# One decode step on one core: the first weight matrix in two loads, 16 partitions and 112

## The chip, the core and the metric

The kernel runs on one core of a Trainium2 chip. The metric is device time in microseconds of one execution; several runs are taken and their median is given. Separately, one execution is recorded by the hardware profiler.

## The reference

One token of a transformer block: grouped-query attention against a cache of 16384 positions, then a mixer and an MLP. Cut to what matters here:

```python
x = A_x                                       # (1, 1, 512)
q = layernorm(x) @ wq                         # wq: 512 x 4096, 32 heads of 128
k, v = repeat(k_cache, 4), repeat(v_cache, 4) # each (8, 16384, 128), bf16
p = softmax(q k^T / sqrt(128));  o = p v
h = x + o @ wo                                # wo: 4096 x 512
c = gelu(layernorm(layernorm(h)) @ w1); ...   # mixer: a shift in time and w2
x1 = ...
out = h + x1 + gelu(layernorm(x1) @ w3) @ w4  # w3: 512 x 1792, w4: 1792 x 512
```

With one token the mixer's shifts leave only zeros, so w1 and w2 are not loaded. The keys and values are 32 MB each and wq, wo are 4 MB each: nearly all the work is to bring bytes from device memory.

## The kernel before

Every operation is noted by a small class, `Program`, with the engine, the tiles that it reads and writes, and, for loads, a semaphore by name. `emit` then writes each engine's instructions in the order noted, with a wait wherever an operation needs a result of another engine or of a load (L101 is the line of the waits). So the order on each engine's queue is the order in the source. `load` (its DMA is issued at L225) puts a load on SP's queue, unless told otherwise; only the token itself, `x4`, is loaded by ACT.

The tiles: `kb` holds keys, 128 partitions by 64 KB, in two halves `kb[0]` and `kb[1]`; `vb` holds values, 128 by 64 KB; `kt` holds one half of the keys transposed. wq has no tile of its own: `wq_sb` is `vb`, whose first half holds wq until the first values come. Partition p of wq_sb gets rows 4p to 4p+3 of wq, which lie one after the other in memory: 32 KB a partition.

The heads are taken in four pairs j. For each pair and half y, DVE transposes the keys in eight pieces (L397) from `kb[y]` into `kt`, PE computes scores (L405), and when both halves are done comes the softmax (L416 to L437) and the product with the values (L448), gathered by DVE (L459, L462). `load_keys(j + 1, y)` is noted after the transposes of pair j, and SP waits at L101 until they are done; pair 1 is loaded as a whole. `load_values(j + 1)` waits for L448 of pair j. The loads of wo, w3 and w4 follow into `kb`.

At the start SP issues wq, then the two halves of the first keys, with no wait. Beside them ACT loads the token, DVE and POOL make constants, and the layernorm of the token is computed on DVE; its end is `xn` (L345). L378 are the 32 matmuls of the projection: they read `xn` and wq, 64 output partitions and 512 columns each, contracting over the 128 partitions, so that every one needs all partitions of wq. L382 and L388 bring the queries into the layout of the scores. `load_values(0)` stands behind: SP waits for the last of the L378 matmuls, since values overwrite wq. In the last pair and after it PE runs some spare matmuls (`spin`, L262) whose results are not used.

In the kernel before, the load of wq writes the key "v", the key of the loads of the values too.

## Time and profile before

| | |
|---|---|
| median of 3 runs | 191.53 us (191.33 to 191.57) |
| profiled execution, its own time | 191.19 us |
| its span, first to last instruction | 189.9 us |
| PE, DVE busy | 122.6 us (65%), 115.8 us (61%) |
| moved from device memory | 79.17 MB, mean 417 GB/s over the span |
| chain that ended last, by engine | DMA 61%, DVE 31%, PE 4% |
| wq: issue to landing | 4096 KB, 12.2 us |

The span is cut into 40 slices of 4.75 us. A digit gives the busy share in tenths; the GB/s row is what the 16 DMA engines of the core moved in that slice. In the chain, each line is a start, a duration and the work that held the end back then. An entry such as "DVE kt<-kb L397" names the engine, the tile written and the tile read.

### The profile page before, as it was taken

The numbers are of one execution on the slowest core, as the hardware profiler recorded it, in microseconds if no ns is written. First come the engines' busy times: TensorE is split into PE (matmuls) and PEld (weight loads), VectorE is DVE, ScalarE is ACT, GpSimd is POOL, SyncE is SP. The second block draws the span as 40 slices with busy tenths as digits, with TensorE's granted clock in tenths as the row PEclk, the third lists the DMA queues.
The fourth block names the chain that finished last, engine by engine and source line by source line (L and its number), as shares of the span: only waits on it lengthen the run. The fifth ranks groups of instructions, "written<-read, shape, count | busy, mean of one in ns | idle before, by whom it ended". The sixth has DMA issues, their size and how long they took to land.

```text
span 189.9 us, 1730 instructions
## 1 busy us (share of the span) xinstructions
PE 122.6 (65%) x726; PEld 45.9 (24%) x726; DVE 115.8 (61%) x176; ACT 9.4 (5%) x16; POOL 7.0 (4%) x15
## 2 busy tenths in 40 slices
PE   0129099693085004999449599944929998779893
PEld 0114033221032001342123222212313422334231
DVE  7755597993502007999450999935079897514274
ACT  3000000002000000000110000011000000500011
POOL 7100000000000000000000000000000000000032
PEclk9999969999558555799956999996575999999999
DMA  6999999999999999997999999999999999989992
GB/s 221 442 442 442 442 442 444 442 442 431 442 442 442 428 442 442 442 442 342 442 435 428 456 442 414 390 442 414 442 442 442 469 431 414 442 368 409 433 408 84
DMA packets 2610, 79.26 MB, mean 417 GB/s; under 512 B 298, under 2 KB 428, under 8 KB 556
## 3 DMA queue, kind: packets, MB, share of 16 engines
q1 hardware_dynamic: 2594, 79.17, 97.2%
q8 instruction: 5, 0.08, 0.2%
q14 instruction: 1, 0.01, 0.0%
q10 hardware_dynamic: 10, 0.00, 0.0%
HBM read 79.17 MB, written 0.00 MB: 417 GB/s over the span
## 4 chain that ended last, share of the span: by engine, by line
DMA 61%; DVE 31%; PE 4%; issue 1%; SPq 1%; ACT 1%; ACTq 0%
DMA kb<-in_A_k_cache_dram 46%; DVE kt L397 28%; DMA kb<-in_B_w_dram 14%; PE O_ps L448 3%; DVE pt L433 1%; SPq L225 1%; DVE mx L416 1%; ACT p_sb L429 1%; DVE od L462 1%; PE s_ps L405 1%; PE mn_ps L571 0%; DVE fin L577 0%; PE mn_ps L423 0%; PE mn_ps L419 0%; DVE od L459 0%
## 5 line engine op out<-in xcount | busy, mean ns | idle before, releaser
L405 PE MATMUL s_ps<-kt,qb 128*128 128x512 bf16 x256 | 69.5, 411 | 24.4 <-DVE kt L397 21.6
L397 DVE STREAM_TRANSPOSE kt<-kb 128x1024 int32<-128x1024 int32 x64 | 72.8, 1206 | 16.7 <-DMA kb<-in_A_k_cache_dram 16.7
L405 PEld LDWEIGHTS s_ps<-kt,qb 128*128 128x128 bf16 x256 | 22.8, 102 | 70.2 <-DVE kt L397 45.7
L448 PE MATMUL O_ps<-vb,pt 128*32 128x512 bf16 x256 | 21.9, 517 | 10.7 <-DMA vb<-in_A_v_cache_dram 6.3
L459 DVE TENSOR_SCALAR od<-O_ps,rowc 128x128 f32<-128x128 f32 x4 | 1.4, 350 | 28.0 <-PE O_ps L448 28.0
L448 PEld LDWEIGHTS O_ps<-vb,pt 128*32 128x32 bf16 x256 | 8.9, 125 | 22.5 <-issue 11.0
L433 DVE STREAM_TRANSPOSE pt<-p_sb 64x1024 bf16<-64x1024 bf16 x8 | 9.9, 1240 | 5.4 <-ACT p_sb L429 5.3
L262 PE MATMUL O_ps<-kt,qb 128*128 128x512 bf16 x52 | 12.9, 380 | 0.0
L429 ACT ACTIVATE p_sb<-s_ps,bias 128x1024 bf16<-128x1024 f32 x4 | 4.5, 1114 | 156.5 <-DVE nmh L425 156.5
L416 DVE TENSOR_REDUCE mx<-s_ps 128x1 f32<-128x1024 f32 x4 | 4.9, 1225 | 4.5 <-PE s_ps L405 4.5
L378 PE MATMUL O_ps<-vb,xn 128*64 128x512 bf16 x16 | 3.6, 631 | 5.8 <-DMA vb<-in_A_wq_dram 5.8
L315 POOL TENSOR_SCALAR st<-st 128x1 f32<-128x1 f32 x1 | 0.2, 244 | 177.5 <-DVE st L300 177.5
L262 PEld LDWEIGHTS O_ps<-kt,qb 128*128 128x128 bf16 x52 | 4.5, 99 | 6.0 <-issue 1.8
L465 PE MATMUL A_ps<-od,zz 128*128 128x128 f32 x8 | 2.0, 326 | 5.1 <-DVE od L462 5.1
L437 PE MATMUL A_ps<-acc,zz 128*128 128x1 f32 x8 | 1.6, 271 | 5.3 <-ACT p_sb L429 5.3
L462 DVE SCALAR_TENSOR_TENSOR od<-O_ps,rowc,od 128x128 f32<-128x128 f32 x12 | 4.2, 351 | 0.4
L419 PE MATMUL mn_ps<-ident_f,mx 128*1 128x128 f32 x8 | 1.5, 271 | 4.4 <-DVE mx L416 4.4
L337 DVE CAST quarter<-ident_f 4x128 bf16<-4x128 f32 x1 | 3.9, 3904 | 0.6 <-POOL ident_f L332 0.6
L339 PE MATMUL O_ps<-x,quarter 4*128 4x128 bf16 x1 | 0.3, 282 | 5.7 <-DVE quarter L337 5.7
L382 DVE STREAM_TRANSPOSE qcol<-O_ps 128x256 f32<-128x256 f32 x4 | 1.6, 428 | 3.9 <-PE O_ps L378 3.9
L378 PEld LDWEIGHTS O_ps<-vb,xn 128*64 128x64 bf16 x16 | 1.4, 167 | 7.2 <-DVE zz L367 5.9
L516 DVE COPY osum<-O_ps 128x512 f32<-128x512 f32 x1 | 0.7, 691 | 3.7 <-PE O_ps L509 3.7
(87 smaller groups left out, 50.9 us busy)
## 6 DMA issues: line engine op xcount, KB each, us to landing
kb<-in_A_k_cache_dram SPq DMA_DIRECT2D x6, 4096.0 KB, 23.5
vb<-in_A_wq_dram SPq DMA_DIRECT2D x1, 4096.0 KB, 12.2
kb<-in_A_wo_dram SPq DMA_DIRECT2D x1, 3072.0 KB, 27.2
kb<-in_B_w_dram SPq DMA_DIRECT2D x1, 1792.0 KB, 24.2
kb<-in_B_w_dram SPq DMA_DIRECT2D x1, 1280.0 KB, 27.0
kb<-in_A_wo_dram SPq DMA_DIRECT2D x1, 1024.0 KB, 29.2
kb<-in_B_w_dram SPq DMA_DIRECT2D x1, 384.0 KB, 27.4
kb<-in_B_w_dram SPq DMA_DIRECT2D x1, 128.0 KB, 27.3
```

The costliest lines, as they stand in the source:

```text
L225: P.op(by, lambda e: e.dma_start(dst, src), w=[key, *also], dma=name)
L262: pe(lambda e: e.matmul(O_ps[out][:, :], qb[:, 0, 0, 0:128], kt[:, 0:512], start=True, stop=True), r=["qb", ("kt", 0)], w=[("O", out)], ba ...
L337: dve(lambda e: e.tensor_copy(quarter[:, :, :], ident_f[0:4, 0:4].unsqueeze(2).to_broadcast([4, 4, 32])), r=["ident_f"], w=["quarter"])
L378: pe(lambda e, row=row, k=k, g=g, at=at: e.matmul(row[64 * g:64 * g + 64, :], copies(xn[:, k:k + 1], 64), wq_sb[:, at:at + REP * DH], star ...
L397: dve(lambda e, view=view: e.transpose(view(kt), view(kb[y])), r=[("r", y, n) for n in range(RPARTS)], w=[("kt", t)])
L405: pe(lambda e, n=n, c=c: e.matmul(s_ps[:, y, :], qb[:, n, j, QPAD - 4 * c:QW - 4 * c], ktv[:, n // 2, n % 2, :, 8 * c:8 * c + 8, :], start ...
L416: dve(lambda e: e.tensor_reduce(mx[:, :], s_all, AX.X, ALU.max), r=[("s", 0), ("s", 1)], w=["mx"], **both)
L429: act(lambda e: e.activation(p_sb[:, :], s_all, ACTF.Exp, bias=bias[:, 0:1], scale=float(SCALE), accum_out=acc[:, :]), r=[("s", 0), ("s", ...
L433: dve(lambda e, g=g: e.transpose(pt[64 * g:64 * g + 64, :, :, g, :], p_sb[64 * g:64 * g + 64, :]), r=["p"], w=["pt"])
L448: pe(lambda e, q=q, ct=ct, xl=xl, ch=ch: e.matmul(O_ps[j % 2][32 * ct:32 * ct + 32, :], pt[:, xl, ch, :, :].rearrange("p g u -> p (g u)"), ...
L462: dve(lambda e, block=block, c=c: e.scalar_tensor_tensor(od[:, :], block, rowc[:, c:c + 1], od[:, :], ALU.mult, ALU.add), r=[key, "rowc", ...
L465: pe(lambda e: e.matmul(A_ps[:, 0:128], zo[:, 96 - 32 * j:224 - 32 * j], od[:, :], start=False, stop=(j == PAIRS - 1), skip_group_check=True),
```

## The change

wq comes by two loads of SP in place of one: the first brings partitions 0 to 15, the second partitions 16 to 127. Both have semaphores and keys of their own. The projection matmuls wait for both; the loads of the values are marked as writing over both.

```diff
+WQ = ((0, 16), (16, 128))
...
         def load_values(j):
-            load("v", vb[:, :], pair_rows(A_v_cache, j), "v")
+            load("v", vb[:, :], pair_rows(A_v_cache, j), "v", also=[("wq", 0), ("wq", 1)])
...
-        load("wq", wq_sb[:, 0:NCH * HQ * DH], A_wq.rearrange("(p k) c -> p (k c)", k=NCH), "v")
+        wq_in = A_wq.rearrange("(p k) c -> p (k c)", k=NCH)
+        for n, (lo, hi) in enumerate(WQ):
+            load(f"wq{n}", wq_sb[lo:hi, 0:NCH * HQ * DH], wq_in[lo:hi, :], ("wq", n))
...
-                        start=(k == 0), stop=(k == NCH - 1)), r=["xn", "v"], w=[key], bank=[key])
+                        start=(k == 0), stop=(k == NCH - 1)), r=["xn", ("wq", 0), ("wq", 1)], w=[key], bank=[key])
```

The order of instructions on PE, DVE, ACT and POOL stays as it was; SP's queue has one load more, right behind the first.

## The prediction

> **What bounds the kernel now.** I read the page's transfer rows first, then the chain that ended last, then the start of the timeline, and last a table of small windows over the first two microseconds. The slices of the page:

> ```profile
> DMA  6999999999999999997999999999999999989992
> GB/s 221 442 442 442 442 442 444 442 442 431 442 442 442 428 442 442 442 442 342 442 435 428 456 442 414 390 442 414 442 442 442 469 431 414 442 368 409 433 408 84
> ...
> q1 hardware_dynamic: 2594, 79.17, 97.2%
> ...
> vb<-in_A_wq_dram SPq DMA_DIRECT2D x1, 4096.0 KB, 12.2
> ```

> From the second slice to the last but one the 16 DMA engines are busy, at the same 442 GB/s for wq, keys and values, whatever the compute engines do. 79.17 MB at 442 GB/s is 179.1 us of the span of 189.9. The rest is a head, where nothing moves yet, and a tail of compute. The chain says the same with the order of things:

> ```profile
> 0.72 0.40 SPq L225
> 1.12 0.06 issue
> 1.17 0.42 SPq L225
> 1.59 0.05 issue
> 1.64 31.49 DMA kb<-in_A_k_cache_dram
> 33.15 9.14 DVE kt L397 x8
> ...
> 160.02 27.42 DMA kb<-in_B_w_dram
> ...
> 187.48 0.64 PE mn_ps L571 x8
> 188.14 0.41 DVE fin L577
> ```

> The first link is SP's issue of the wq load, then that of the keys. A piece of keys issued at 1.64 lands 31.49 us later, not because it is slow but because 4 MB of wq and 4 MB of keys stand ahead of it on the same engines. DVE's transposes (L397) wait for those landings, and all later loads wait for the buffers that DVE and PE give back. Nowhere in the middle does the stream run dry (DMA share 7 to 9 tenths in every slice), so a delay of the stream at its head has no gap to disappear in: it arrives at the end in full. The same holds for a gain. And a load has landed only when the slowest of the 16 engines has brought its share, so it is the slowest lane that counts. The windows show the head:

> ```profile
> 1.60:1.70 0.10, 0.00 (x0) 0.00 (x0) 0.01 (x1) 0.10 (x1) 0.10 (x2) 1.00 0.04 8
> 1.70:1.80 0.10, 0.00 (x0) 0.00 (x0) 0.10 (x1) 0.10 (x1) 0.10 (x1) 1.00 6.32 1641
> ...
> 1.90:2.00 0.10, 0.00 (x0) 0.00 (x0) 0.10 (x1) 0.10 (x1) 0.10 (x1) 1.00 3.49 983
> ```

> The last two columns are the DMA share and GB/s; a packet is counted whole where it starts, so shares above 1 are rows that begin there. wq's rows begin from about 1.7, some 0.6 us after SP finished issuing at 1.12, and all lanes have begun by about 2.1.

> **The unit of the sum.** wq is 4096 KB, 128 rows of 32 KB, 8 rows to an engine. At 442 GB/s it takes 9.49 us, so one row on one lane takes 9.49 / 8 = 1.19 us (27.6 GB/s a lane). I call that a row-time.

> **Part by part.** *One more issue on SP.* The rows of L225 on SP last 0.33 to 0.43 us, so the second wq load goes out at about 1.6, and the two key loads at 1.64 and 2.1 move back by some 0.45 us. Behind them SP has nothing until the value load at 18.88. The cover is the wq transfer itself, 9.49 us: the keys' rows cannot start before it is through. The first load alone holds each lane one row-time, to about 2.9, and the second load's rows should be there by 1.6 + 0.6 = 2.2. Cost zero; without that cover, 0.45 us.

> *One more completion.* Each load ends with one small marker on each lane. The page has 2594 packets on the queue for 18 loads by SP, and 442 GB/s holds across loads of 4 MB and 8 MB alike, so a marker costs too little to see: zero, at most 0.05 us.

> *The extra wait on PE.* L378's first matmul waits for two loads instead of one. Behind it on PE stand the 32 projection matmuls, and DVE's L382 and SP's value load wait for them. The larger load lands last on the lanes, so the wait for the small one is over by then: zero. SP's value load waits for the same L378 matmuls as before.

> *Earlier first bytes.* Bounded by the head: the wq issue took 0.398 us against 0.328 for most others, and rows begin 0.6 us after it. If a load of 16 rows is prepared faster than one of 128, at most about 0.4 us is won; at least nothing. I take 0, since short and long loads (the 128 KB one too) show issues of 0.33 to 0.43.

> *Where the 16 rows land.* This decides. Every load so far writes all 128 partitions, so the trace shows 442 GB/s only for transfers spread over the whole width of SBUF. The change sends 16 engines at 16 neighbouring partitions, an eighth of the width. If the 27.6 GB/s of a lane is a limit of the engine or of the source, the 16 rows take one row-time, 1.19 us, and nothing changes. If it is a limit of the place of landing, and an eighth of the partitions takes an eighth of the rate, they take 8 row-times, 9.49 us. These are the ends from the rows. That the rate is the same 442 for 32 KB rows of keys and 64 KB rows of values, from different tensors and beside any compute, speaks for a fixed width on this side of the transfer. Whole loads run evenly with eight rows to a lane, so the nearest reading of these rows is 16 entries of one lane-rate, each serving the eight partitions of one lane. How the eight are grouped no row shows: as eight neighbours the 16 rows meet on two entries (9.49 us), as two groups of four on four entries, four lanes to each (4 row-times, 4.75 us), as pairs on eight (2.4 us). [...]

> [...] It ends at 4 + 11 = 15 row-times instead of 8. The loads behind it are even again, so it catches nothing up and stays 7 row-times late: 7 x 1.19 = 8.3 us. [...] The least under any sharing by four is 4 row-times (the 12 untouched entries still have 8 rows each, after the first 4): 4.7 us. In pairs the first load loses one row-time and the second little: 1.2 us or more. Lanes that start unevenly can drag each other for up to about five row-times more: some 14 us.

> **Sum.** 0 + 0 + 0 + 8.3 on the profiled execution's 191.19 us (span 189.9 and 1.3 around it) is 199.5; on the median of the runs, 191.53, it is 199.8. Own range 196 to 206.

> **Rivals.** (1) *Faster: the limit is not at the landing, and the small load starts the stream sooner.* For it: 0.6 us lie between issue and first row, and the stream's start is on the chain, so a gain is kept to the end. Against it: issues cost the same at every size. It decides if a lane writes anywhere at 27.6 GB/s; then the time is 191.53 less up to 0.4, some 191.2, or unchanged. (2) *It doesn't do what it says:* the rows are given to engines by where they land, so four engines take four rows each and the second load gives these four fewer. All lanes then carry 8 rows as before and the time stays at 191.5. [...] (3) *Only the first load pays:* the 112 rows run evenly, 3 row-times lost, 191.5 + 3.6 = 195.1. [...] (4) *The 112 rows are dealt in turn,* so every step lands on 16 neighbours: 8 steps lose 3 row-times each, 28.6 us, 220.

> **Chances.** Forecast 0.55, rival 1 0.15, rival 2 0.12, rival 3 0.10, rival 4 0.08. A measurement can tell about 0.2% here, 0.4 us. Rival 1 splits into faster 0.06, same 0.06, slower 0.03 (small costs without the gain); rival 2 into 0.03, 0.05, 0.04. So faster 0.09, same 0.11, slower 0.80. The range reaches from rival 1 (191.0) to the forecast's upper end (206) and leaves out rival 4 and tails.

> **What would show it.** In the changed profile: the first slice or two of GB/s far below 442 (about 110 for the first 4.75 us of the stream, then uneven), the middle at 442 again; 19 loads on SP, issue about 0.4 us each; L378 waiting for wq until about 21 instead of 13.1, and every later landing late by the same amount; near the end a stretch in which some lanes are already idle, so DMA share below 9 there. Wrong if the slices read 442 from the second on and L378 starts near 13: then the limit is not at the landing. If L378 starts 3.6 us late, the second load is even; if the low rate lasts over 30 us, rival 4.

## The result, and the profile after

The changed kernel takes 200.37 us (median of 4 runs, 199.94 to 200.52); the kernel before, run beside it, 191.46 us (191.33 to 191.57). The ratio is 1.0463, with a 95% interval of 1.0446 to 1.0481. The profiled execution took 200.52 us with a span of 199.2, where the kernel before had 191.19 and 189.9: 9.3 us more in both; the medians lie 8.9 us apart.

The page of the changed kernel, the slices and the two loads of wq (issue to landing is the last number):

```profile
DMA  7999999999999999999899999999999999989992
GB/s 105 211 309 217 349 454 434 434 436 421 424 421 421 474 500 434 434 421 421 345 434 421 447 487 421 434 424 395 428 434 421 493 464 434 434 349 396 423 413 94
...
vb<-in_A_wq_dram SPq DMA_DIRECT2D x1, 3584.0 KB, 21.6
...
vb<-in_A_wq_dram SPq DMA_DIRECT2D x1, 512.0 KB, 6.7
```

A slice is now 4.98 us long. In the first five, some 25 us, the engines are as busy as ever (digits 7 and 9) but move only 105 to 349 GB/s. From the sixth slice on most slices read 421 to 454, much as before the change. The digits count an engine as busy while a row is under way, however slowly it goes, so DMA share alone would have shown nothing. The same head in windows, first of the kernel before, then of the changed kernel; the last columns are DMA share and GB/s, with a row counted where it begins:

```profile
1.70:2.70 1.00, 0.00 (x0) 0.00 (x0) 1.00 (x1) 0.99 (x2) 1.00 (x1) 1.00 1.93 525
2.70:3.50 0.80, 0.00 (x0) 0.00 (x0) 0.80 (x1) 0.11 (x1) 0.80 (x1) 1.00 0.00 0
3.50:4.20 0.70, 0.00 (x0) 0.00 (x0) 0.70 (x1) 0.00 (x0) 0.70 (x2) 1.00 1.73 749
4.20:4.70 0.50, 0.00 (x0) 0.00 (x0) 0.50 (x1) 0.00 (x0) 0.50 (x1) 1.00 0.00 0
4.70:5.40 0.70, 0.00 (x0) 0.00 (x0) 0.70 (x1) 0.00 (x0) 0.70 (x1) 1.00 1.73 749
```

```profile
1.70:2.70 1.00, 0.00 (x0) 0.00 (x0) 1.00 (x1) 0.99 (x2) 1.00 (x1) 1.00 3.64 525
2.70:4.00 1.30, 0.00 (x0) 0.00 (x0) 1.30 (x1) 0.11 (x1) 1.30 (x2) 1.00 0.00 0
4.00:5.00 1.00, 0.00 (x0) 0.00 (x0) 1.00 (x1) 0.00 (x0) 1.00 (x1) 1.00 0.00 0
```

525 GB/s through one microsecond is 0.525 MB, sixteen rows of 32 KB, and so is 749 through 0.7. In the kernel before, every lane begins a second row between 3.5 and 4.2 and a third between 4.7 and 5.4. The rows follow each other every 1.2 us, but the first one, begun at about 1.7 and followed from about 3.6 on, takes some 1.9: the stream has a slow start of about 0.7 us. In the changed kernel all 16 lanes begin their row of the small load just as early. Then none begins another for over two microseconds (the next sixteen begin between 5.0 and 6.0), so each of these rows takes much longer than 1.19 us. Over the second load and behind it, again in windows of the changed kernel:

```profile
8.00:22.00 14.00, 0.00 (x0) 0.00 (x0) 3.73 (x20) 0.00 (x0) 0.00 (x0) 1.00 1.02 262
22.00:28.00 6.00, 5.14 (x26) 2.57 (x28) 1.56 (x4) 0.00 (x0) 0.00 (x0) 1.00 0.99 426
```

262 GB/s through most of the 112 rows, the full rate as soon as the first keys follow. Smaller windows of the changed kernel show how the lanes go through these rows:

```profile
8.20:8.70 0.50, 0.00 (x0) 0.00 (x0) 0.43 (x4) 0.00 (x0) 0.00 (x0) 1.00 4.52 1049
8.70:10.40 1.70, 0.00 (x0) 0.00 (x0) 1.49 (x8) 0.00 (x0) 0.00 (x0) 1.00 0.00 0
10.40:10.90 0.50, 0.00 (x0) 0.00 (x0) 0.46 (x3) 0.00 (x0) 0.00 (x0) 1.00 3.73 1049
10.90:12.30 1.40, 0.00 (x0) 0.00 (x0) 1.19 (x8) 0.00 (x0) 0.00 (x0) 1.00 0.00 0
...
19.60:20.30 0.70, 0.00 (x0) 0.00 (x0) 0.00 (x0) 0.00 (x0) 0.00 (x0) 1.00 0.00 0
20.30:21.80 1.50, 0.00 (x0) 0.00 (x0) 0.00 (x0) 0.00 (x0) 0.00 (x0) 1.00 1.25 350
```

1049 GB/s through half a microsecond are sixteen rows again, and so are 350 through 1.5. All 16 lanes begin a row, and none begins its next until all have begun this one. That happens seven times, and then the first rows of the keys begin, between 20.3 and 21.8. The seven steps last 15.2 us (5.1 to 20.3), 2.2 each where an even row takes 1.2.

What this delays, in the timelines of the kernel before and of the changed kernel, and then in their chains (of the chain before one line, 72.38):

```profile
13.09 3.62 PE L378 MATMUL O_ps<-vb,xn 128*64 128x512 bf16 x16 [5.84 <-DMA vb<-in_A_wq_dram]
```

```profile
22.86 3.63 PE L381 MATMUL O_ps<-vb,xn 128*64 128x512 bf16 x16 [15.61 <-DMA vb<-in_A_wq_dram]
```

```profile
72.38 18.15 DVE kt L397 x16
```

```profile
1.15 0.40 SPq L226
...
2.07 40.07 DMA kb<-in_A_k_cache_dram
42.16 9.14 DVE kt L400 x8
...
81.72 18.15 DVE kt L400 x16
...
159.28 9.14 DVE kt L400 x8
...
196.81 0.64 PE mn_ps L574 x8
197.47 0.41 DVE fin L580
```

The lines of the code have moved by three, so L381 is the old L378 and L400 the old L397. The projection starts at 22.86 instead of 13.09, 9.8 us late. The transposes at 81.72, against 72.38 before, are 9.3 us late, and so is the last MLP matmul (196.81 against 187.48). The chain runs through the same links, with one more issue by SP at its start. The delay is 9.0 us at the first transposes (42.16 against 33.15) and 9.3 at the end, so nothing of it is made up on the way.

### The profile page after: what moved, and what is told of

It reads as the page before. It is cut to its first block, busy times and chain, and to the rows that moved or that the text cites. A ratio compares the mean times of both kernels' runs of the same rounds, so it can differ in the third digit from the quotient of the medians.

```text
span 199.2 us, 1728 instructions
## 1 busy us (share of the span) xinstructions
PE 121.2 (61%) x723; PEld 45.5 (23%) x726; DVE 115.8 (58%) x176; ACT 9.4 (5%) x16; POOL 7.0 (4%) x15
## 3 DMA queue, kind: packets, MB, share of 16 engines
q1 hardware_dynamic: 2610, 79.17, 97.3%
HBM read 79.17 MB, written 0.00 MB: 397 GB/s over the span
## 4 chain that ended last, share of the span: by engine, by line
DMA 63%; DVE 30%; PE 4%; issue 1%; SPq 1%; ACT 1%; ACTq 0%
DMA kb<-in_A_k_cache_dram 49%; DVE kt L400 27%; DMA kb<-in_B_w_dram 14%; PE O_ps L451 3%; DVE pt L436 1%; SPq L226 1%; DVE mx L419 1%; ACT p_sb L432 1%; DVE od L465 1%; PE s_ps L408 1%; PE mn_ps L574 0%; DVE fin L580 0%; PE mn_ps L426 0%; PE mn_ps L422 0%; DVE od L462 0%
## 5 line engine op out<-in xcount | busy, mean ns | idle before, releaser
L408 PE MATMUL s_ps<-kt,qb 128*128 128x512 bf16 x256 | 69.2, 407 | 25.0 <-DVE kt L400 21.8
L400 DVE STREAM_TRANSPOSE kt<-kb 128x1024 int32<-128x1024 int32 x64 | 72.8, 1206 | 17.0 <-DMA kb<-in_A_k_cache_dram 17.0
L408 PEld LDWEIGHTS s_ps<-kt,qb 128*128 128x128 bf16 x256 | 22.3, 101 | 71.0 <-DVE kt L400 48.0
L451 PE MATMUL O_ps<-vb,pt 128*32 128x512 bf16 x256 | 20.1, 482 | 10.7 <-DMA vb<-in_A_v_cache_dram 6.5
L381 PE MATMUL O_ps<-vb,xn 128*64 128x512 bf16 x16 | 3.6, 632 | 15.6 <-DMA vb<-in_A_wq_dram 15.6
L451 PEld LDWEIGHTS O_ps<-vb,pt 128*32 128x32 bf16 x256 | 8.3, 117 | 21.3 <-DMA vb<-in_A_v_cache_dram 9.3
L263 PE MATMUL O_ps<-kt,qb 128*128 128x512 bf16 x49 | 12.3, 380 | 0.4 <-issue 0.3
L381 PEld LDWEIGHTS O_ps<-vb,xn 128*64 128x64 bf16 x16 | 1.5, 167 | 17.0 <-issue 17.0
L381 PE MATMUL s_ps<-vb,xn 128*64 128x512 bf16 x16 | 3.1, 551 | 0.0
## 6 DMA issues: line engine op xcount, KB each, us to landing
kb<-in_A_k_cache_dram SPq DMA_DIRECT2D x6, 4096.0 KB, 26.6
```

The lines of the kernel that those rows point to most:

```text
L263: pe(lambda e: e.matmul(O_ps[out][:, :], qb[:, 0, 0, 0:128], kt[:, 0:512], start=True, stop=True), r=["qb", ("kt", 0)], w=[("O", out)], ba ...
L381: pe(lambda e, row=row, k=k, g=g, at=at: e.matmul(row[64 * g:64 * g + 64, :], copies(xn[:, k:k + 1], 64), wq_sb[:, at:at + REP * DH], star ...
L400: dve(lambda e, view=view: e.transpose(view(kt), view(kb[y])), r=[("r", y, n) for n in range(RPARTS)], w=[("kt", t)])
L408: pe(lambda e, n=n, c=c: e.matmul(s_ps[:, y, :], qb[:, n, j, QPAD - 4 * c:QW - 4 * c], ktv[:, n // 2, n % 2, :, 8 * c:8 * c + 8, :], start ...
L451: pe(lambda e, q=q, ct=ct, xl=xl, ch=ch: e.matmul(O_ps[j % 2][32 * ct:32 * ct + 32, :], pt[:, xl, ch, :, :].rearrange("p g u -> p (g u)"), ...
```

## Experiments

All times are medians beside the kernel before, which gave 191.43 to 191.48 us. A row-time is 1.19 us, as in the prediction.

### The price of 16 neighbouring partitions by itself

One load was put ahead of the kernel before, into kt, which has no content yet. The whole of wq follows in one load. Two theories are set against each other in this and the next kernels. The landing theory: 16 rows into 16 neighbouring partitions take four row-times, 4.75 us, which puts this kernel at about 196.2 us. The four was the author's estimate; no row of the kernel before shows it. The source theory: 16 rows side by side in memory are read slowly, wherever they land.

```diff
+        wq_in = A_wq.rearrange("(p k) c -> p (k c)", k=NCH)
+        load("pre", kt[0:16, :], wq_in[0:16, :], "pre", also=[("kt", t) for t in range(8)])
         load("wq", wq_sb[:, 0:NCH * HQ * DH], A_wq.rearrange("(p k) c -> p (k c)", k=NCH), "v")
```

> The kernel before with one more load ahead of wq: the first 16 rows of wq into partitions 0 to 15 of kt, which is unused then (it is overwritten later). wq itself stays one load of 128 partitions. At the even rate 16 rows cost one row-time, 1.19 us. [...] Source theory (16 rows side by side in memory are read slowly, wherever they land): about 196 too. If a lane writes anywhere at its full rate: 192.7.

195.47 us, ratio 1.0212 (1.0197 to 1.0227): 4.0 us for 16 rows that at the even rate cost 1.2. So 2.8 us are lost, somewhat less than the three row-times (3.6) of the landing theory; the slow start of 0.7 us, which the kernel before pays too, fits as the cover for the rest.

Then the same with the source rows spread (`wq_in[0:128:8, :]` into `kt[0:16, :]`):

> As near16, but the 16 rows come from every eighth row of wq (256 KB apart) and still land in partitions 0 to 15. Landing theory: the same 4 row-times, 196.2 us. Source theory: the reads are spread, so one row-time, 192.7 us.

195.85 us, ratio 1.0232 (1.0217 to 1.0247). Reading from far apart does not help: it is 0.4 us slower. The source theory falls.

And with the landing spread (`wq_in[0:16, :]` into `kt[0:128:8, :]`):

> As near16 with the same neighbouring source rows, but landing in every eighth partition (0, 8, ... 120). Landing theory with two groups of four: eight entries with two rows each, 2 row-times, 193.8 us. Landing theory with eight straight neighbours to an entry: 16 entries, one row-time, 192.7 us. Source theory: as near16, about 196.

193.75 us, ratio 1.0121 (1.0106 to 1.0136): 2.3 us, about two row-times. The difference is small, but well outside its interval. Some 0.2 us of it lie ahead of the landing: SP's issue took 0.57 us here instead of 0.37 in near16. One row-time and this would be 1.4. So it is the place of landing: the same 16 rows cost 4.0 us in partitions 0 to 15 and 2.3 us in every eighth. The 2.3 is near the two row-times that the landing theory has with groups of four, and far from the one that it has with straight groups of eight. Which partitions share an entry is not shown. The issue rows of the three kernels, in this order, say it a second time; the last number is issue to landing of the same 512 KB:

```profile
kt<-in_A_wq_dram SPq DMA_DIRECT2D x1, 512.0 KB, 6.7
```

```profile
kt<-in_A_wq_dram SPq DMA_DIRECT2D x1, 512.0 KB, 7.3
```

```profile
kt<-in_A_wq_dram SPq DMA_DIRECT2D x1, 512.0 KB, 4.8
```

With 512 KB over all 128 partitions (the cut by columns, below) it is 3.6 us. 4.8 is one row-time more, 6.7 and 7.3 are 2.6 and 3.1 more: one, two (with the later start) and about four row-times to land.

### The price of the other 112 by itself

```diff
+        wq_in = A_wq.rearrange("(p k) c -> p (k c)", k=NCH)
+        load("pre", kt[16:128, :], wq_in[16:128, :], "pre", also=[("kt", t) for t in range(8)])
```

> The kernel before with one more load ahead of wq: rows 16 to 127 of wq into partitions 16 to 127 of kt. At the even rate 7 row-times, 8.3 us: 199.8 us. [...] Source theory: these rows are read spread over 3.5 MB, so the even 199.8 us.

205.88 us, ratio 1.0769 (1.0725 to 1.0814): 14.4 us, 12.1 row-times, where 7 are needed at the even rate. The loss is 14.4 - 8.3 = 6.1 us. With near16's 2.8 that makes 8.9 us, as much as the whole change: 200.37 - 191.46 = 8.9. That it agrees to the tenth is luck, since the interval here reaches nearly 0.9 us to either side. Which lane brings which row, no run shows.

### Other cuts of wq

The changed kernel with `WQ = ((0, 64), (64, 128))`:

> The changed kernel with the cut at partition 64: two loads of 64 neighbouring partitions. [...] If only a small first load or blocks of seven cost something: 191.5, as before.

201.96 us, ratio 1.0552 (1.0536 to 1.0568). It loses 10.5 us, though both loads are of 2 MB. Its slices:

```profile
GB/s 203 202 209 202 235 444 477 431 511 418 408 418 431 418 418 418 431 418 444 428 451 431 418 509 418 418 421 411 431 418 424 444 421 457 509 304 423 420 412 91
```

Four slices at 202 to 209 GB/s, somewhat under half of the full rate: on half of the partitions a load got about half of the rate here. At half of the even rate wq would take 16 row-times instead of 8, 9.5 us more; the 10.5 measured are near that.

The changed kernel with `WQ = ((0, 112), (112, 128))`:

> [...] If the two prices only add up as in near16 and extra112 (2.8 and 6.1 us over the even rate), with the 16 rows no longer under the slow start (0.7 us more): 191.4 + 9.6 = 201.0. [...] All lanes in lock step (two row-times for each of the seven steps, four for the last): 18 row-times, 203.3.

201.03 us, ratio 1.0492 (1.0467 to 1.0517). The two prices add up in this order too. It is 0.7 us slower than the change, as it would be if the slow start no longer covers the 16 rows; but the intervals of the two ratios overlap, so the 0.7 alone is not shown.

The changed kernel, cut by columns instead of partitions:

```diff
-WQ = ((0, 16), (16, 128))
+WQ = ((0, 2048), (2048, 16384))
...
-            load(f"wq{n}", wq_sb[lo:hi, 0:NCH * HQ * DH], wq_in[lo:hi, :], ("wq", n))
+            load(f"wq{n}", wq_sb[:, lo:hi], wq_in[:, lo:hi], ("wq", n))
```

> The changed kernel, but wq is cut by columns: the first 4 KB of every partition (512 KB as in the change, over all 128 partitions), then the other 28 KB. Landing theory: both loads reach all 16 entries with a lane to each, nothing is lost: 191.5 us, and at most 0.4 less if a first load of less data starts the stream sooner. If a small first load is itself the cost (two loads, two waits, a longer start): 2 us or more slower.

191.30 us, ratio 0.9997 (0.9988 to 1.0005): no difference. Two lines of its page:

```profile
GB/s 243 447 414 441 441 441 443 441 441 431 441 441 441 441 428 441 441 441 341 441 441 435 497 441 414 362 414 414 441 441 441 469 445 428 428 385 391 425 413 73
...
vb<-in_A_wq_dram SPq DMA_DIRECT2D x1, 512.0 KB, 3.6
```

It has the same number of loads, waits and issues as the change, and the same 512 KB ahead. All of these cost nothing that can be measured. Nor does a small first load start the stream sooner by anything that reaches the end.

### Do slow lanes hold back the others?

The prediction's 11 row-times for the second load are an estimate that lets each lane run on by itself. Two kernels look at how lanes go that land on a part of the partitions: two loads of 16 rows ahead of wq, into every fourth partition. In one kernel both loads go to the same partitions, in the other the second load goes to others.

```diff
-            load("v", vb[:, :], pair_rows(A_v_cache, j), "v")
+            load("v", vb[:, :], pair_rows(A_v_cache, j), "v", also=["pre1"])
...
+        wq_in = A_wq.rearrange("(p k) c -> p (k c)", k=NCH)
+        load("pre0", kt[16:77:4, :], wq_in[0:16, :], "pre0", also=[("kt", t) for t in range(8)])
+        load("pre1", vb[16:77:4, NCH * HQ * DH:], wq_in[0:16, :], "pre1")
```

This is same_lanes_twice; in other_lanes_then the last line writes to `vb[48:109:4, NCH * HQ * DH:]`.

> The kernel before with two more loads of 16 rows ahead of wq, both into every fourth partition from 16 to 76 (kt, then the free half of vb). [...] If a full entry holds back all 16 lanes alike: two row-times a load, 4 in all, 4.75 us: 196.2. At the even rate 2.4 us: 193.9.

> [...] All lanes held back alike: 4 row-times, 196.2, the same as same_lanes_twice.

196.24 us (ratio 1.0261, 1.0247 to 1.0276) and 195.98 us (1.0245, 1.0231 to 1.0259). The two lie 0.26 us apart, and both stand at the 196.2 of two row-times a load. The slices of the two kernels, in this order, are nearly one row:

```profile
GB/s 216 303 431 431 431 438 444 527 431 421 431 431 431 431 431 431 431 431 431 333 431 431 431 518 431 421 431 350 431 431 431 512 421 431 431 345 424 416 410 90
```

```profile
GB/s 216 323 431 431 431 431 431 527 431 421 431 431 431 431 431 431 431 431 431 334 431 431 431 519 431 421 431 350 431 431 431 512 421 431 431 345 423 416 408 96
```

Which lanes meet in either kernel is not shown, so the 0.26 alone does not tell how the lanes go. Windows of same_lanes_twice do:

```profile
2.00:2.60 0.60, 0.00 (x0) 0.00 (x0) 0.60 (x1) 0.59 (x1) 0.60 (x1) 1.00 3.46 874
2.60:3.80 1.20, 0.00 (x0) 0.00 (x0) 1.20 (x1) 0.20 (x1) 1.20 (x2) 1.00 0.00 0
3.80:4.60 0.80, 0.00 (x0) 0.00 (x0) 0.80 (x1) 0.00 (x0) 0.80 (x1) 1.00 3.20 655
4.60:6.40 1.80, 0.28 (x1) 0.10 (x1) 1.39 (x4) 0.00 (x0) 0.92 (x1) 1.00 0.00 0
6.40:7.15 0.75, 0.49 (x2) 0.49 (x2) 0.52 (x3) 0.00 (x0) 0.00 (x0) 1.00 2.13 699
```

The windows with a rate begin sixteen rows each: the first load, the second, and the first rows of wq. All lanes have begun their second row by 4.6. A lane at 1.2 us a row would be through with it by 5.8 and begin one of wq. None does before 6.4: all 16 lanes are held back, none goes at the even rate. Whether slow ones hold back the others, or each lane is slow by itself, the runs don't show.

In the changed kernel too the lanes go through the 112 rows step by step, as its windows above show. But a step there is not simply two row-times: that would be 14 row-times for the seven, and extra112 took 12.1, while last16 came 2.3 us short of its lock-step time. What sets the length of such a step stays open.

## Why the prediction was right, and where it was not

*The bound and the carry* held. The stream of loads sets the time; a delay at its head, 9.8 us at the projection and 9.0 at the first transposes, is 9.3 us at the end, with no gap in between to take it up.

*The unit* was 2% too small. A slice of 4.75 us in which every lane begins four rows reads 442 GB/s, because rows are counted where they begin. Longer windows of the kernel before read less: 431 GB/s from 33 to 72 us and 432 from 72 to 123.6. At 432 a row-time is 1.21 us, not 1.19; that moves the forecast by 0.2 us. (And the head was read a little short: one of the sixteen lanes begins only after 2.5 us, not by 2.1.)

*The small costs* (one more issue, marker and wait, an earlier start) were put at zero, and the cut by columns, which has all of them and nothing else, shows 0.9997. The markers of one more load are 16 more packets under 512 B (314 against 298 on the page). This is also the end of the rival that a small load starts the stream sooner.

*The landing* was the term that decides, and the four row-times were right in kind: spread sources gain nothing (195.85 us against 195.47), and landing in every eighth partition costs 2.3 us instead of 4.0. The four itself no run shows; near16 showed 4.0 us, 3.4 row-times, for the 16 rows. The rival by which four engines would bring four rows each falls with the first window: 16 rows begin within one microsecond, one on each lane.

*The two sizes* were off in opposite directions, and the sum, 8.3 us forecast and 8.9 measured, hides it; that it came so close is in part luck. The first load was put at 3.6 us lost and lost 2.8. The slow start of 0.7 us, which the prediction did not set against this term, fits the difference. The second was put at four row-times lost, 4.75 us, and lost 6.1. The step that failed is the estimate of 11 row-times for the 112 rows. No run shows the 11, the time of a slowest lane where each runs on by itself; extra112 showed 12.1. By that estimate the lanes end apart; the changed kernel shows them in step: all 16 begin the row behind the second load between 20.3 and 21.8, after seven steps of 2.2 us, and in same_lanes_twice no lane goes on before 6.4. Behind the second load the stream is at 426 GB/s at once, and the last slices of its DMA row (9, 9, 9, 2) are those of before, where I had expected lanes that fall idle early. All lanes are late together. The prediction did allow up to five row-times for lanes that drag each other, without a working for it, and no run shows the five; extra112 shows about one, 12.1 where the estimate has 11.

*The other rivals.* That only the first load pays would have been 195.1; near16 alone is at 195.5, but the 112 rows pay more than the 16, and the projection is 9.8 us late, not 3.6. Rows dealt in turn would have kept the rate low for over 30 us; it is back at 22.

## What to carry to other kernels

In these runs a load had the full rate (442 GB/s in most slices of the kernel before, 441 in the cut by columns) only when it went to all 128 partitions; 16 rows into every eighth partition still cost 2.3 us where 1.2 is even. So if a load has to be cut, cut it by columns, which cost nothing here, and not by partitions, which cost 8.9 to 10.5 us. In a kernel that loads bound, read the GB/s row beside the DMA digits: an engine whose row goes slowly counts as busy (digits of 9 at 211 to 349 GB/s here). Where the stream never ran dry, the delay of the first load was paid in full at the end (9.0 us at the first transposes, 9.3 at the end).
